# A transformer layer with Strassen products on one core: copies of stacked left rows on every second partition, and a row of attention pieces per FFN pair

## The chip, the cores and the metric

One core of a Trainium2 chip. TensorE (PE) multiplies, VectorE (DVE) and ScalarE (ACT) work elementwise, GpSimd (POOL) and SyncE (SP) mostly issue DMA transfers; ACT issues some too. The metric is the time of one launch in microseconds (us).

## The reference

`x` is [2048, 576], with D = 576, 32 heads of 18, and an FFN of F = 4608:

```python
xn = _layernorm(x, axis=-1)
return x + _A_ref(xn, A_wqkv, A_wo) + _B_ref(xn, B_w1, B_b1, B_w2, B_b2)
# _A_ref: each row s attends to rows s, s-2, ..., s-14 (W, dil = 8, 2) of its head, softmax, then @ wo
# _B_ref: relu(xn @ w1 + b1)**2 @ w2 + b2
```

Everything is float32.

## The kernel before

**Numbers.** TensorE takes the operands as pairs of a high part and a low part; each product is the sum of three (high·high, high·low, low·high). ACT makes the high part by a copy, DVE the low part by a subtraction.

**Blocks.** The 2048 rows are four blocks of 512, taken in two pairs: half `s` = 0 holds blocks 0 and 1, half `s` = 1 blocks 2 and 3. The first FFN product (and QKV) of two blocks is made by seven products in place of eight: sums and differences of weight blocks (the tiles `w1s`) times sums and differences of x (`SS`, printed as `S`, and `X`). A "pair" `p` is two of the 36 tiles of 128 FFN columns; each half has 18 pairs (`NP`), and `ffn_pair(s, p, work)` writes one of them out. `phase_a(0)` and `phase_a(1)` run the pairs of a half; within a pair stand, at fixed places, the seven products (L698, output `p`), some products with w2 of a pair before (`work`, L590), the splitting of weights into high and low (`w2s`, `w1s`), and the sums that turn seven products into four results (`r`, `h`). After `phase_a(1)`, `phase_blocks` makes the second FFN product of the odd pairs in 28 steps (L1514), and `phase_b1` the rest.

**Left rows.** 576 is four times 128 and 64 over. For pairs 0 to 2 (`PLAIN` = 3) the 64 left rows are multiplied on their own (`left`, L704, with the last slot of `w1s`). From pair 3 on, the product of the left rows is one matmul of 128 partitions more for each of the seven ("stacked"): 32 high rows and 32 low rows of x, each row twice, against the weights' high and low rows, each twice in another order, so that the 128 partitions hold the pairings of high and low. `left_x` makes x's rows and stores them in a scratch array in DRAM, `stscr[s]`, printed as `stk`: 64 rows, high and low in turn (`2 * NS * TB` from one high row to the next). `load_stack` (its transfer is L636) brings them into spare tiles: for `s` = 0 into `kv`, `xf` and `x4d`, for `s` = 1 into two buffers of `w1r`, of 4 and 3 of the seven places. Each call starts two transfers of 64 partitions: the first fills partitions 0 to 63 with the 64 rows, the second partitions 64 to 127 with the same rows. `left_w` makes the weights' rows and stores them in `lw` (L652): first 32 high rows, then 32 low rows; `load_left_weights` (L663) reads each of those 64 rows twice in succession onto 128 partitions.

**Queues.** SP issues the stack loads, the loads of `lw` and of w2 (`w2r`) and the stores; in `phase_a(1)` ACT issues the loads of `w1s` (L536, two transfers to a pair, 1024 and 768 KB), one pair ahead of use, into three buffers.

**Attention.** It has 16 items (four blocks by four groups), each a generator of 19 steps: four times a product (`pr<-q,kv`) and a reduction (`lg<-pr`), then the maximum and its subtraction (`mx`, `lg<-lg,mx`), after which the generator stops with "exp"; then the exponential on ACT (L414); the sum, reciprocal and scaling (`sm`, `lg<-lg,sm`); then four times a product (`pr<-lg,kv`) and a step of three additions (`pr<-pr` twice and `q<-pr`). Nearly all of it is on DVE. The order of every engine's instructions is the order in which the program is written, and `side(k)` puts the next k steps at the place where it is called. Three tables say how many: `PIECES[p]`, one number for each pair of `phase_a(0)`, all at the pair's start; `SPOTS[p]`, six numbers for each pair of `phase_a(1)`, one for each of its places (`spot(0)` to `spot(5)`); `LAST[k]` after step k of `phase_blocks`. In `phase_a(1)` the number is added to `owed`, and steps are run until less than half a step is owed or an "exp" is met; what an "exp" stops is owed to the next place. Places 2 and 3 of a pair lie beside its two sums `r<-p,r`, on which the next products wait.

Of the kernel before, what the change touches and what calls it, by code (L numbers as in the profile page):

```python
# [8 lines left out]
F32 = mybir.dt.float32  # L9
# [7 lines left out]
P = 128  # L17
S, D, F = 2048, 576, 4608
H, DH, W, DIL = 32, 18, 8, 2
TB = 512  # L20
# [5 lines left out]
G = 4  # L26
# [6 lines left out]
L = P // G  # L33
# [9 lines left out]
NS = 7  # L43
PLAIN = 3
ROWS = {(4 * b - 1 + k // 3, k % 3): (b, h) for b in (2, 3) for k, h in ((0, 0), (2, 2), (3, 1), (5, 2), (6, 2))}
PIECES = (0, 0, 0, 2, 3, 4, 0, 3, 2, 0, 2, 2, 1, 0, 2, 2, 4, 5)
SPOTS = ('000001',) + ('110022', '110023', '110023', '110023') * 4 + ('110021',)
QUADS = ('01111110111110', '10100010101011', '00110111111111', '10010000111111', '00000000000001', '00110010101010')
LAST = '0000000000000111001010111111'
SINGLES = '12121212121200000000'  # L50
PAIRED = tuple(range(1, 16, 2))
SINGLE = tuple(p for p in range(NP) if p not in PAIRED)
# [7 lines left out]
def block_kernel(ctx: ExitStack, tc: tile.TileContext, x, xt, wqkv, wo, w1, b1, w2, b2, w1l, w2q, w2l, out):  # L60
    nc = tc.nc
# [53 lines left out]
    stscr = [dram.tile([2 * L, NS, TB], F32, name=f"stk{s}") for s in range(2)]  # L115
    lwscr = [dram.tile([G, 2, L, NS * P], F32, name=f"lw{i}") for i in range(-(-NP // G))]
# [10 lines left out]
    def tt(out, a, b, op):  # L127
        return nc.vector.tensor_tensor(out=out, in0=a, in1=b, op=op)  # L128
# [312 lines left out]
    def side(k, exp=True):  # L441

        while k > 0:
            if current[0] is None:
                if not queue or queue[0][0] not in landed:
                    return k
                name, make = queue.pop(0)
                current[:] = [make(), None, name]
                steps_done[0] = 0
            if current[1] == "exp" and not exp:  # L450
                return k
            try:
                current[1] = next(current[0])
                steps_done[0] += 1
                k -= 1
            except StopIteration:
                current[0] = None
        return 0
# [3 lines left out]
    def some_side(t):  # L462
        owed[0] += t
        while True:
            exp = current[1] == "exp"
            cost = COST[steps_done[0]] if current[0] is not None else COST[0]
            if owed[0] < cost / 2 or side(1):
                break
            owed[0] -= cost
            if exp or current[1] == "exp":  # L470
                break
# [128 lines left out]
    def dims(t, off, *ap):  # L600
        a = t[tuple(slice(0, 1) for _ in t.shape)]
        return bass.AP(tensor=a.tensor, offset=a.offset + off, ap=[*ap])

    def high_low(v, store):
        lo, hi = v[:, :NS], v[:, NS:]
        yield
        nc.scalar.activation(hi.bitcast(F32R), lo, AF.Copy)
        yield
        tt(lo.bitcast(F32R), lo, hi, ALU.subtract)
        store(0, hi)  # L610
        store(1, lo)
        yield
# [20 lines left out]
    def load_stack(s, t, i):  # L633
        n = min(t.shape[1], NS - i)
        for h in range(2):
            nc.sync.dma_start(t[2 * h * L:2 * (h + 1) * L, :n].bitcast(F32), stscr[s][:, i:i + n])  # L636
        for k, place in STACK.items():
            if i <= place < i + n:
                ST[k] = t[:, place - i]
# [5 lines left out]
    def left_w(i):  # L645
        v = rv.pop(("w", i))
        w = lambda k: v[:, STACK[k]]
        tt(w(T3), w(B22), w(T1), ALU.subtract)
        tt(w(T1), w(T1), w(B11), ALU.subtract)
        tt(w(T2), w(B22), w(T1), ALU.subtract)  # L650
        tt(w(T4), w(B21), w(T2), ALU.subtract)
        yield from high_low(v, lambda k, part: (nc.gpsimd if i else nc.sync).dma_start(  # L652
            dims(lwscr[i], k * L * NS * P, [NS * P, L], [2 * L * NS * P, G], [1, NS * P]), part.rearrange("p s c -> p (s c)")))

    def load_left_weights(s, p):
        place = (p - PLAIN) % 2 + 1 if not s else (p - PLAIN) % 3
# [16 lines left out]
    def ffn_pair(s, p, work, first=False):  # L673
# [32 lines left out]
        def part(i):  # L706
# [15 lines left out]
            if i == 2 - p and p in (1, 2) and s:  # L722
                load_stack(1, sb.tile([P, 4, TB], F32R, name="w1r", bufs=2), 4 * p - 4)
            if i == 2 and p == PLAIN - 1 and not s:
                load_stack(0, mt.tile([P, 1, TB], F32R, name="x4d"), 6)
# [7 lines left out]
            if (p, i) == (1, 2):  # L733
                load_stack(0, sb.tile([P, 5, TB], F32R, name="kv", bufs=3), 0)
                load_stack(0, sb.tile([P, 1, TB], F32R, name="xf"), 5)
            r = p // G + 1
            if i == 1 and p % G == 1 and G * r < NP:
                load_left_w(r, sb.tile([P, 2 * NS, P], F32, name="st"))
            elif p % G == 2 and G * r < NP:
                if i == 0:  # L740
                    rv["of", r] = left_w(r)
                next(rv["of", r])
# [50 lines left out]
        def spot(i):  # L793
            if s and (not first or i == 5):
                some_side(int(SPOTS[p][i]))

        if not first and not s:
            side(PIECES[p], False)
        spot(0)
# [276 lines left out]
    def load_h(s, p):  # L1076
        t = hs[s, p] = mt.tile([P, 2, 2, TB], F32R, name="h", bufs=3)
        nc.sync.dma_start(t[:, 1].rearrange("p f t -> p (f t)").bitcast(F32), hscr[s][p])
# [6 lines left out]
    def h_lo(s, p):  # L1085
        if p < NP:
            t = hs[s, p]
            tt(t[:, 1], t[:, 1].bitcast(F32), t[:, 0].bitcast(F32), ALU.subtract)
# [415 lines left out]
    def phase_blocks():  # L1504
# [28 lines left out]
        for k in range(len(ORDER)):  # L1533
# [54 lines left out]
            if k == 25:  # L1588
                load_h(1, SINGLE[1])
                h_hi(1, SINGLE[0])  # L1590
                h_lo(1, SINGLE[0])
            side(int(LAST[k]))
        load_h(1, SINGLE[2])
# [253 lines left out]
    def q0():  # L1847
# [59 lines left out]
        for j in range(NJ):  # L1907
# [5 lines left out]
            if j in (0, 2):  # L1913
                some(parts, 2)
        of_w = left_w(0)
        hi(B11, b11)
        some(parts, 2)
# [174 lines left out]
```

## Time and profile before

| | |
|---|---|
| time before, median of 3 runs | 1099.99 us (1099.34 to 1100.98) |
| the profiled execution's own time | 1099.84 us |
| its span in the trace | 1098.1 us |
| TensorE busy | 99% of the span |
| VectorE busy | 85% |
| ScalarE busy | 52% |
| GpSimd busy | 15% |
| moved by DMA | 312.53 MB, mean 285 GB/s |

The span is from the first to the last event that the profiler saw, 1.74 us less than the execution's own time. Busy shares are averages over the whole span. The list of waits says for each engine which instructions stood still and what ended the wait; the windows give each engine's busy time, the clock granted to TensorE (PEclk, 1.00 is full speed) and the DMA rate in a stretch of the span; the timeline gives single instructions with their start, their duration and, in brackets, the idle time before them and what ended it. Consecutive instructions of one kind stand in one row (x6) with the time of all of them.

### The profile page before, as it was taken

How to read it: one execution, taken by the hardware profiler on the slowest of the kernel's cores; microseconds unless marked ns; L12 is line 12 of the kernel's file. 1: busy time of each engine (PE TensorE's matmuls, PEld its weight loads, DVE VectorE, ACT ScalarE, POOL GpSimd, SP SyncE). 2: the span in 40 equal slices, each digit the busy share in tenths (PEclk: the TensorE clock that was granted, in tenths of full speed). 3: DMA queues.
4: the chain of work that ended last, by engine and by line, in shares of the span. 5: the costliest groups of instructions: out<-in, count | busy, mean ns of one | idle time of the engine just before them, and what ended most of it. 6: DMA issues, size and time to landing. Idle time of an engine off the chain costs nothing.

```text
span 1098.1 us, 13935 instructions
## 1 busy us (share of the span) xinstructions
PE 1083.5 (99%) x4871; PEld 908.9 (83%) x4871; DVE 930.9 (85%) x1245; ACT 570.7 (52%) x800; POOL 160.0 (15%) x294
## 2 busy tenths in 40 slices
PE   9999999999999999999999998999999999999998
PEld 7998888888888888888799986888778888887887
DVE  7976899999988979999899676879688888888986
ACT  5545655666656564555344344555455555543332
POOL 5011220212130100003110301021021040000110
PEclk9999999999999999999999999999999999999999
DMA  8758997897998697876865989998988988566573
GB/s 284 256 198 304 302 403 275 320 356 285 328 342 311 222 387 238 282 247 219 304 219 164 359 299 308 383 334 333 377 291 327 361 322 313 177 206 213 203 235 100
DMA packets 106887, 312.53 MB, mean 285 GB/s; under 512 B 12865, under 2 KB 39489, under 8 KB 95169
## 3 DMA queue, kind: packets, MB, share of 16 engines
q1 hardware_dynamic: 70048, 198.75, 51.5%
q0 software_dynamic: 15584, 71.96, 18.0%
q10 hardware_dynamic: 21184, 40.94, 11.1%
q8 instruction: 38, 0.62, 0.2%
q14 instruction: 33, 0.26, 0.1%
HBM read 216.62 MB, written 94.98 MB: 284 GB/s over the span
## 4 chain that ended last, share of the span: by engine, by line
PE 90%; DVE 5%; DMA 3%; issue 1%; ACT 1%; POOL 0%; ACTq 0%; DVEq 0%; POOLq 0%
PE p L590 35%; PE p L698 34%; PE p L1187 9%; PE p L1514 6%; PE p L1843 2%; DMA w1s<-w 2%; PE p L1191 2%; DVE pr L128 1%; PE p L1898 1%; PE p L704 1%; DMA w2r<-in_wo 1%; DVE h L128 1%; PE p L1753 1%; DVE w2s L128 0%; DVE r L128 0%
## 5 line engine op out<-in xcount | busy, mean ns | idle before, releaser
L590 PE MATMUL p<-h,w2s 128*128 128x512 f32 x1618 | 389.6, 390 | 0.0
L590 PEld LDWEIGHTS p<-h,w2s 128*128 128x128 f32 x1618 | 303.7, 188 | 64.3 <-ACT h L749 0.5
L698 PE MATMUL p<-X,w1s 128*128 128x512 f32 x864 | 219.6, 390 | 1.5 <-DVE r L128 1.5
L698 PEld LDWEIGHTS p<-X,w1s 128*128 128x128 f32 x864 | 162.2, 188 | 35.8 <-DVE r L128 1.9
L698 PE MATMUL p<-S,w1s 128*128 128x512 f32 x648 | 167.2, 394 | 0.5 <-ACT p L786 0.5
L698 PEld LDWEIGHTS p<-S,w1s 128*128 128x128 f32 x648 | 121.1, 189 | 29.3 <-ACT r L806 2.9
L562 ACT ACTIVATE w2s<-w2r 128x640 fp32r<-128x640 f32 x132 | 96.7, 734 | 87.2 <-PE p L590 54.1
L434 POOL DMA_DIRECT2D o<-q x128 | 69.4, 620 | 466.3 <-DVE q L128 465.8
L128 DVE TENSOR_TENSOR w2s<-w2r,w2s 128x576 fp32r<-128x576 f32 (+1 forms) x133 | 99.8, 751 | 18.0 <-ACT w2s L562 17.8
L745 ACT ACTIVATE r<-r,b1t 128x512 f32<-128x512 f32 x72 | 52.1, 724 | 116.1 <-DVE r L128 114.1
L128 DVE TENSOR_TENSOR h<-h 128x1024 fp32r<-128x1024 f32 (+1 forms) x74 | 72.5, 989 | 21.3 <-ACT h L762 13.7
L128 DVE TENSOR_TENSOR pr<-lg,kv 128x1152 f32<-128x1152 f32 x64 | 86.7, 1355 | 1.3
L128 DVE TENSOR_TENSOR pr<-q,kv 128x1152 f32<-128x1152 f32 x64 | 86.7, 1355 | 1.1
L405 DVE TENSOR_REDUCE lg<-pr 128x64 f32<-128x1152 f32 x64 | 86.4, 1350 | 1.0
L128 DVE TENSOR_TENSOR r<-p,r 128x512 f32<-128x512 f32 (+2 forms) x81 | 55.0, 681 | 36.2 <-ACT r L831 18.2
L128 DVE TENSOR_TENSOR pr<-pr 128x576 f32<-128x576 f32 (+1 forms) x128 | 77.5, 605 | 3.1
L753 ACT ACTIVATE r<-r 128x1024 f32<-128x1024 f32 x56 | 59.2, 1057 | 0.9
L806 ACT ACTIVATE r<-p 128x512 f32<-128x512 f32 x36 | 21.5, 598 | 57.2 <-PE p L698 57.1
L128 DVE TENSOR_TENSOR w1s<-w1r,w1s 128x1024 fp32r<-128x1024 f32 (+2 forms) x42 | 46.2, 1102 | 5.6 <-ACT w1s L523 5.0
L831 ACT ACTIVATE r<-p 128x512 f32<-128x512 f32 x36 | 21.5, 599 | 54.1 <-PE p L698 54.1
L745 ACT ACTIVATE r<-p,b1t 128x512 f32<-128x512 f32 x72 | 48.2, 671 | 0.0
L128 DVE TENSOR_TENSOR h<-r,h 128x1024 fp32r<-128x1024 f32 (+2 forms) x35 | 39.9, 1146 | 7.6 <-ACT r L753 6.0
(263 smaller groups left out, 1488.2 us busy)
## 6 DMA issues: line engine op xcount, KB each, us to landing
kv<-kvq POOLq DMA_DIRECT2D x32, 1296.0 KB, 9.6
w2r<-in_w SPq DMA_DIRECT2D x112, 320.0 KB, 4.1
w<-w1s SPq DMA_DIRECT2D x21, 1024.0 KB, 7.1
w1s<-w ACTq DMA_DIRECT2D x19, 1024.0 KB, 8.0
h<-r SPq DMA_DIRECT2D x28, 512.0 KB, 6.5
h<-h SPq DMA_DIRECT2D x28, 512.0 KB, 4.0
w<-w1s SPq DMA_DIRECT2D x15, 768.0 KB, 9.4
w1s<-w ACTq DMA_DIRECT2D x15, 768.0 KB, 7.7
```

Of the source, the lines that this page charges most:

```text
L128: return nc.vector.tensor_tensor(out=out, in0=a, in1=b, op=op)
L405: nc.vector.tensor_reduce(out=lg[:, j * HG:(j + 1) * HG].rearrange("p a w -> p w a"), in_=pr.rearrange("p w (a d) -> p w a d", d=DH), axis ...
L434: nc.gpsimd.dma_start(rows[:, i], q[i * L:(i + 1) * L, :, a:z])
L562: nc.scalar.activation(w2s[stream[i]][:, :DE], raw2[i], AF.Copy)
L590: nc.tensor.matmul(yp[b][c], v, a, start=c not in yb[b], stop=c in last and c not in [o[0] for o in ops[i + 1:]], skip_group_check=True)
L698: nc.tensor.matmul(to, l, r, start=start and i == 0, stop=i == len(mm) - 1, skip_group_check=True)
L745: nc.scalar.activation(to, a, AF.Relu, bias=b1t[:, f:f + 1])
L753: nc.scalar.activation(r, r, AF.Square)
L1187: nc.tensor.matmul(to, l[:, js], r, start=start and n == 0, stop=n == len(mm) - 1, skip_group_check=True)
L1191: nc.tensor.matmul(to, v[:, js], ws[LEFT, f][:, n], start=False, stop=n == 1, skip_group_check=True)
L1514: nc.tensor.matmul(p, l, r, start=id(p) not in begun, stop=stop, skip_group_check=True)
L1843: nc.tensor.matmul(p[:, :QW], l, r, start=k == 0, stop=k == len(mm) - 1)
```

## The change

The transfers of `load_stack` are put together in another way. The first now takes the 32 high rows and writes each of them to two neighbouring places of every second partition (0, 2, 4, ...), the second the 32 low rows to partitions 1, 3, 5, ... A transfer still covers 64 partitions with the same bytes, but its partitions now span all 128. The weights' rows are stored high and low in turn, so that the same rows meet in the matmul; the loads of `lw` are as before. The products are the same, in another order of the 128 rows.

Besides, three tables of attention's steps change: pair 14 of `phase_a(0)` gets one step more, `SPOTS` has a row of its own for each pair in place of four rows repeated, and step 22 of `phase_blocks` gets none.

```diff
-PIECES = (0, 0, 0, 2, 3, 4, 0, 3, 2, 0, 2, 2, 1, 0, 2, 2, 4, 5)
-SPOTS = ('000001',) + ('110022', '110023', '110023', '110023') * 4 + ('110021',)
+PIECES = (0, 0, 0, 2, 3, 4, 0, 3, 2, 0, 2, 2, 1, 0, 3, 2, 4, 5)
+SPOTS = ('000002', '110022', '110023', '010023', '110023', '110022', '110023', '100024', '010024', '120022', '110023', '110023', '110023', '110022', '110023', '110023', '110123', '010021')
...
-LAST = '0000000000000111001010111111'
+LAST = '0000000000000111001010011111'
...
     def load_stack(s, t, i):
         n = min(t.shape[1], NS - i)
         for h in range(2):
-            nc.sync.dma_start(t[2 * h * L:2 * (h + 1) * L, :n].bitcast(F32), stscr[s][:, i:i + n])
+            nc.sync.dma_start(t[h::2, :n].rearrange("p s c -> p (s c)").bitcast(F32),
+                              dims(stscr[s], h * NS * TB + i * TB, [2 * NS * TB, L], [0, 2], [1, n * TB]))
...
         yield from high_low(v, lambda k, part: (nc.gpsimd if i else nc.sync).dma_start(
-            dims(lwscr[i], k * L * NS * P, [NS * P, L], [2 * L * NS * P, G], [1, NS * P]), part.rearrange("p s c -> p (s c)")))
+            dims(lwscr[i], k * NS * P, [2 * NS * P, L], [2 * L * NS * P, G], [1, NS * P]), part.rearrange("p s c -> p (s c)")))
```

How the instructions stand on SP's queue around the second half's stack (`stk_151` is its scratch array), before:

```order
L551 DMA w2r<-in_w 128x640
L636 DMA w1r<-stk_151 64x2048 x2
L663 DMA st<-lw_152 128x1x896
L636 DMA w1r<-stk_151 64x1536 x2
L766 DMA op_157<-h 128x2048
```

and of the change:

```order
L551 DMA w2r<-in_w 128x640
L636 DMA w1r<-stk_151 64x1x2048 x2
L664 DMA st<-lw_152 128x1x896
L636 DMA w1r<-stk_151 64x1x1536 x2
L767 DMA op_157<-h 128x2048
```

Nothing moves: the four transfers keep their places and sizes, and only the partitions they write and the rows they read differ.

On VectorE, from the last part of pair 9 of `phase_a(1)` into pair 10 (`r_6718` and `r_6717` are pair 9's two sums, as `r_6720` and `r_6719` are in the change; `h<-h x2` finishes pair 9 in the course of pair 10), before:

```order
L128 TENSOR_TENSOR w2s<-w2r,w2s 128x576
L128 TENSOR_TENSOR r_6718<-p_6659,r_6698 128x512
L411 TENSOR_REDUCE mx<-lg 128x32
L128 TENSOR_TENSOR lg<-lg,mx 128x256
L128 TENSOR_TENSOR r_6717<-p_6659,r_6698 128x512
L128 TENSOR_TENSOR h<-h 128x512 x2
L416 TENSOR_REDUCE sm<-lg 128x32
L417 RECIPROCAL sm<-sm 128x32
L128 TENSOR_TENSOR lg<-lg,sm 128x256
L128 TENSOR_TENSOR pr<-lg,kv 128x1152
L128 TENSOR_TENSOR pr<-pr 128x576
L128 TENSOR_TENSOR pr<-pr 128x288
```

and of the change:

```order
L411 TENSOR_REDUCE mx<-lg 128x32
L128 TENSOR_TENSOR lg<-lg,mx 128x256
L128 TENSOR_TENSOR w2s<-w2r,w2s 128x576
L128 TENSOR_TENSOR r_6720<-p_6659,r_6698 128x512
L128 TENSOR_TENSOR r_6719<-p_6659,r_6698 128x512
L416 TENSOR_REDUCE sm<-lg 128x32
L417 RECIPROCAL sm<-sm 128x32
L128 TENSOR_TENSOR lg<-lg,sm 128x256
L128 TENSOR_TENSOR pr<-lg,kv 128x1152
L128 TENSOR_TENSOR pr<-pr 128x576
L128 TENSOR_TENSOR pr<-pr 128x288
L128 TENSOR_TENSOR q<-pr 128x144
```

The maximum with its subtraction has moved ahead of the first sum of pair 9, and the sum, reciprocal and scaling with the first product and additions have moved from behind the first `h<-h x2` of pair 10 to ahead of it.

On VectorE in `phase_blocks`, around its steps 21 to 23 (`X_7720`, and `X_7722` in the change, is one sum of outputs; the `w1s<-w1s` is the low part of an operand that a later step takes), before:

```order
L128 TENSOR_TENSOR X_7720<-X_7720 128x1024
L128 TENSOR_TENSOR h<-h 128x1024
L128 TENSOR_TENSOR w1r<-X_7720,w1r 128x1024
L128 TENSOR_TENSOR w2s<-w2r,w2s 128x576
L128 TENSOR_TENSOR pr<-pr 128x576
L128 TENSOR_TENSOR pr<-pr 128x288
L128 TENSOR_TENSOR q<-pr 128x144
L128 TENSOR_TENSOR w1s<-w1s 128x1024
```

and of the change:

```order
L128 TENSOR_TENSOR X_7722<-X_7722 128x1024
L128 TENSOR_TENSOR h<-h 128x1024
L128 TENSOR_TENSOR w1r<-X_7722,w1r 128x1024
L128 TENSOR_TENSOR w2s<-w2r,w2s 128x576
L128 TENSOR_TENSOR w1s<-w1s 128x1024
```

The step of three additions no longer stands ahead of the low part; the place of step 20 holds additions where it held a product of attention.

## The prediction

> **What bounds the kernel now.** I read the shares first, then the list of what TensorE waits for, then the windows around its longest waits, then the timeline inside them.
>
> ```profile
> PE 1083.5 (99%) x4871; PEld 908.9 (83%) x4871; DVE 930.9 (85%) x1245; ACT 570.7 (52%) x800; POOL 160.0 (15%) x294
> ```
> ```profile
> PE p L704 <- DMA w1s<-w: 4.0, 1, 4.0
> ...
> PE p L698 <- DVE r L128: 1.5, 1, 1.5
> PE p L1514 <- DVE w1s L128: 0.7, 1, 0.7
> PE p L698 <- ACT p L786: 0.5, 1, 0.5
> ```
>
> TensorE is busy all but 1% of the span, and the change takes no matmul away. So it can only win where TensorE stands still or runs at a lower clock. Four waits (total us, times, longest us) lie where the change acts: one on a DMA, 4.0 us, and three on DVE or ACT, 2.7 us together. Those at the start, between the halves and at the end lie elsewhere, and I leave them as they are.
>
> The long wait is in the third pair of the second half (pair 2), which is the last one before the stacked rows are used:
>
> ```profile
> 664.16 1.52 PE L698 MATMUL p<-S,w1s 128*128 128x512 f32 x6
> 669.71 0.72 PE L704 MATMUL p<-x,w1s 128*128 128x512 f32 x2 [4.03 <-DMA w1s<-w]
> ```
> ```profile
> 655.71 0.33 ACTq L536 DMA_DIRECT2D w1s<-w  x1
> ```
> ```profile
> w1r<-stk SPq DMA_DIRECT2D x2, 512.0 KB, 14.8
> ```
> ```profile
> 130.00:136.00 6.00, 6.00 (x28) 4.95 (x28) 5.80 (x11) 4.53 (x7) 0.00 (x0) 1.00 0.97 215
> 140.00:147.00 7.00, 7.00 (x32) 5.80 (x31) 6.72 (x12) 4.43 (x6) 0.55 (x1) 1.00 1.02 421
> 543.00:546.00 3.00, 3.00 (x17) 2.88 (x16) 2.96 (x6) 1.35 (x2) 0.00 (x0) 1.00 0.88 330
> 658.00:665.00 7.00, 7.00 (x32) 5.80 (x32) 4.49 (x7) 4.53 (x6) 0.00 (x0) 1.00 1.05 221
> 665.00:670.00 5.00, 0.97 (x5) 0.51 (x4) 4.93 (x8) 0.60 (x1) 0.00 (x0) 1.00 1.00 308
> 670.00:674.00 4.00, 4.00 (x12) 3.10 (x12) 0.02 (x1) 0.00 (x0) 0.00 (x0) 0.57 1.04 259
> ```
>
> The weights that L704 needs are issued at 655.71 and land as the wait ends, at 669.7. In between stand the stack loads (`w1r<-stk`, 14.8 us each to landing). The last three columns of a window are the granted clock, the DMA share and GB/s. While stack loads are in flight (658 to 665, and 130 to 136 in the first half) the engines are as busy as ever, 1.05 and 0.97, but move only 221 and 215 GB/s; from 140 to 147, with other loads, a share of 1.02 moves 421. **A stack load onto 64 neighbouring partitions runs at half the rate.** After the wait TensorE's clock is 0.57 for 4 us, a loss of 4 × 0.43 = 1.72. So the place costs 4.03 + 1.72 = 5.75 us.
>
> [...]
>
> ```profile
> 542.57 1.44 PE L1187 MATMUL p<-r,X 128*128 128x432 f32 x6 [2.04 <-DVE h L1063]
> ```
>
> **The stack's copies.** Number of transfers, bytes and queue places stay. What can change is the rate, and what each row reads: every DRAM row is still read twice, now in succession, as the loads of `lw` do already:
>
> ```profile
> mb<-lw SPq DMA_DIRECT2D x13, 448.0 KB, 5.6
> ```
>
> 448 KB land in 5.6 us there, so reading twice is not slow in itself. From 658 to 669.7 the queues moved 221 × 7 + 308 × 4.7 = 2995 KB. At 421 GB/s these take 7.1 us, and the weights land at 665.1. TensorE is ready for them at 664.16 + 1.52 = 665.68. The wait goes, with 0.6 us in hand, and the clock loss with it: **−5.75**. The break-even rate is 2995 / 7.68 = 390 GB/s. The loads queued behind it come some 4.6 us sooner, and TensorE 5.75 sooner, so the next one loses about 1 us of its lead. The two ends of this term: nothing at 221 GB/s, 5.75 at 390 or above. I take the upper one, nearest to the row of 421.
>
> [...] The slow windows agree with the half rate; no row here has a strided transfer.
>
> The weights' rows leave in the same stores with another step in DRAM, off TensorE's path, and the matmuls are the same: 0.
>
> **Pairs 9 to 11.** A step of attention is a product (1.36), a reduction, or three additions (1.25 + 0.31 = 1.56).
>
> ```profile
> 785.35 1.42 DVE L128 TENSOR_TENSOR h<-h 128x512 f32<-128x512 f32 x2 [4.80 <-ACT h L762]
> 787.97 1.36 DVE L128 TENSOR_TENSOR pr<-lg,kv 128x1152 f32<-128x1152 f32 x1
> 789.36 1.25 DVE L128 TENSOR_TENSOR pr<-pr 128x576 f32<-128x576 f32 x2
> 790.64 0.31 DVE L128 TENSOR_TENSOR q<-pr 128x144 f32<-128x144 f32 x1
> 790.87 1.28 DVE L128 TENSOR_TENSOR h<-h 128x512 f32<-128x512 f32 x2
> 793.34 0.75 DVE L128 TENSOR_TENSOR w2s<-w2r,w2s 128x576 fp32r<-128x576 f32 x1
> 794.01 0.68 DVE L128 TENSOR_TENSOR r<-p,r 128x512 f32<-128x512 f32 x1
> ```
> ```profile
> 791.53 1.75 PE L590 MATMUL p<-h,w2s 128*128 128x512 f32 x7
> 794.75 1.66 PE L698 MATMUL p<-X,w1s 128*128 128x512 f32 x6 [1.47 <-DVE r L128]
> 802.37 1.65 PE L698 MATMUL p<-S,w1s 128*128 128x512 f32 x6 [0.53 <-ACT p L786]
> ```
>
> DVE stood idle for 4.80 us, then had softmax's scaling, two products and additions between its `h` and the sum `r` that TensorE waits for. Of the change, scaling, product and additions stand ahead of 785.35, where that idle time takes them. What is left: 1.42 + 1.36 + 1.28 + 1.56 + 0.75 + 0.68 = 7.05, done at 792.4; TensorE comes at 791.53 + 1.75 = 793.28. So the 1.47 goes, and the 0.53 of pair 11, which descends from it; the first six matmuls after each wait took 1.66 and 1.65 for 1.52, another 0.27: **−2.27**.
>
> What moves ahead is met in pair 9:
>
> ```profile
> 766.15 0.69 DVE L128 TENSOR_TENSOR r<-p,r 128x512 f32<-128x512 f32 x1
> 770.80 1.22 DVE L128 TENSOR_TENSOR h<-r,h 128x1024 fp32r<-128x1024 f32 x1
> 777.23 0.42 DVE L128 TENSOR_TENSOR lg<-lg,mx 128x256 f32<-128x256 f32 x1
> 778.07 1.52 PE L698 MATMUL p<-X,w1s 128*128 128x512 f32 x6
> ```
> ```profile
> L405 DVE TENSOR_REDUCE lg<-pr 128x64 f32<-128x1152 f32 x64 | 86.4, 1350 | 1.0
> ```
>
> From 766.84 DVE has three products and three reductions (8.13), the `h` (1.22), maximum and subtraction (0.84), the low part (0.75) and the sum (0.69): 11.63 without the gaps, so 778.47. TensorE comes at 778.07: a new wait of **+0.4**. Between nothing (ACT or the gaps give it back) and 0.84 (all of the moved step), I take the sum.
>
> **The other places.** In `phase_blocks`:
>
> ```profile
> 1003.85 1.22 DVE L128 TENSOR_TENSOR w1s<-w1s 128x1024 fp32r<-128x1024 f32 x1
> 1005.13 1.42 PE L1514 MATMUL p<-w1s,w1r 128*128 128x512 f32 x5 [0.66 <-DVE w1s L128]
> ```
>
> The additions (1.56) leave from ahead of the low part, so its wait goes, −0.66; at step 20 the additions stand for a product, 0.2 more, which I count in full: **−0.46**. In pair 16 of the second half a product (1.36) comes ahead of the second sum:
>
> ```profile
> 883.78 0.69 DVE L128 TENSOR_TENSOR r<-p,r 128x512 f32<-128x512 f32 x1
> 888.02 0.58 ACT L786 ACTIVATE p<-p 128x512 f32<-128x512 f32 x1
> 889.93 1.52 PE L698 MATMUL p<-S,w1s 128*128 128x512 f32 x6
> ```
>
> ACT's chain behind that sum then ends its copy `p<-p` at 888.60 + 1.36 = 889.96, just as TensorE comes for it: **+0.1**, between 0 and 1.4. Pair 14 of the first half gets the maximum and subtraction (0.84) one pair sooner, and the following pairs have it less; DVE's spare 15% hides it, 0, at most 0.84. The remaining moves of a step by one place even out within a pair, 0, each bounded by its 1.36 either way.
>
> **Sum:** −5.75 − 2.27 − 0.46 + 0.4 + 0.1 = −7.98. From the profiled execution's 1099.84 this is **1091.8**; the median of the runs, 1099.99, is 0.15 above that execution, which I neglect.
>
> **Rivals.**
>
> *The rate rises by a part only.* Sixteen engines share 64 rows, four each. If an engine takes four rows in succession, they now lie on eight neighbouring partitions, and engines that work in step could still meet on the same part of the memory. At 300 GB/s the weights land at 658 + 10.0 = 668.0: a wait of 2.3 without clock loss, so 1091.8 + 2.3 = **1094.1**; at 270 it is 3.4 and the clock is at stake, 1095.2 to 1096.9. For it: the limit lies in something that several partitions share, as the full engine share at half rate shows, and the stride only spreads rows over it. Against it: the spread is even over a whole transfer.
>
> *The change doesn't do what it says.* If DRAM reads of the scratch rows set the 221, or the engines stay in step, the term is 0, and what is left is the tables': −2.23, **1097.6**. For it: both slow windows read the same kind of scratch. Against it: `mb<-lw` reads such rows at no such cost.
>
> *A new wait on DVE takes the rest.* The rows of `SPOTS` were set for a program with the old wait in pair 2; that wait gave DVE and the loads some 6 us of lead. Without it a sum or a load a few pairs later may be late by 2 to 4: about **1095**. For it: DVE is 85% busy, and pair 9 already comes out late by 0.4. Against it: from pair 3 on, 4.80 us of idle time in pair 10 absorb a shift.
>
> *Slower.* If strided rows halve the rate once more, the 1547 KB of 658 to 665 take 14 us in place of 7: the weights land 7 us later, the clock loss stays, 1099.84 + 7 − 2.23 = **1104.6**. It decides from a loss of 4.4 us on, that is under 1547 / 11.4 = 136 GB/s. For it: two neighbouring copies of one row now read DRAM in short succession. Against it: `mb<-lw`, and the row size on either side is unchanged.
>
> **How the numbers follow.** Full rate 0.52, part of it 0.20, no gain in rate 0.17, new wait 0.06, slower 0.05. Forecast 1091.8. The full-rate case alone reaches from 1090.0 (the +0.5 of pairs 9 and 16 and the 0.2 of step 20 do not come, and the loads behind give 1 us) to 1093. With the part rate and the new wait the range is **1090.0 to 1097.2**; outside lie most of the third case and the last. About 0.2%, 2.2 us, is what a measurement can tell from no change. The first, second and fourth cases lie under 1097.8; 1097.6 sits at the border, and half of its 0.17 counts as faster. Faster 0.86, same 0.09, slower 0.05.
>
> **What would show it.** Right: the wait at L704 under 0.5 us, no clock below 1.00 in the 4 us behind it, the stretch after the stack loads' issue at 400 GB/s or more, and `w1r<-stk` landing in under 11 us; no wait of pair 10 on `r`; the `w1s` wait of `phase_blocks` gone; a new wait of about 0.4 in pair 9. Wrong: 215 to 221 GB/s again while only stack loads are in flight, a wait of 4 us on `w1s<-w`, or a new wait of over 1 us on `r` or `p` in the second half.

## The result, and the profile after

The changed kernel takes 1089.88 us (median of 4 runs, 1088.06 to 1090.64) where the kernel before took 1099.95 (4 runs, 1099.34 to 1100.98): a ratio of 0.9905, with a 95% interval of 0.9888 to 0.9922. The forecast was 1091.8 with a range of 1090.0 to 1097.2. The direction was right and the gain, 10.1 us where 8.0 were forecast, was underestimated, so that the time lies 0.1 us below the range. The profiled execution of after is the fastest of the four, 1088.06 us with a span of 1086.3.

The shares of the page, and the list of what TensorE waits for:

```profile
PE 1080.5 (99%) x4871; PEld 908.2 (84%) x4871; DVE 932.3 (86%) x1245; ACT 571.2 (53%) x800; POOL 160.3 (15%) x294
```
```profile
PE p L1671 <- DVE lg L1664: 2.1, 1, 2.1
```

Of TensorE's waits in before one is left, that at the start. (Line numbers behind `load_stack` are one higher in the changed kernel, so L704 is L705.) Pair 2 of the second half in the timeline, TensorE, then the queues of ACT and SP:

```profile
661.89 1.52 PE L699 MATMUL p<-S,w1s 128*128 128x512 f32 x6
663.25 0.61 PE L705 MATMUL p<-x,w1s 128*128 128x512 f32 x2
```
```profile
651.44 0.60 ACT L832 ACTIVATE r<-p 128x512 f32<-128x512 f32 x1 [2.12 <-PE p L699]
651.44 0.33 ACTq L536 DMA_DIRECT2D w1s<-w  x1
```
```profile
651.46 3.53 SPq L636 DMA_DIRECT2D w1r<-stk  x2
```

The two matmuls of L705 come without a wait. The list of DMA issues (us to landing last) and the windows (granted clock, DMA share, GB/s last) show the rate:

```profile
w1r<-stk SPq DMA_DIRECT2D x2, 512.0 KB, 9.9
```
```profile
655.00:658.00 3.00, 3.00 (x15) 2.49 (x14) 2.23 (x4) 1.54 (x3) 0.00 (x0) 1.00 0.99 415
658.00:661.00 3.00, 3.00 (x15) 2.46 (x15) 1.91 (x3) 2.40 (x4) 0.00 (x0) 1.00 1.02 421
661.00:665.00 4.00, 4.00 (x19) 3.34 (x18) 3.21 (x6) 1.88 (x3) 0.00 (x0) 1.00 1.03 419
665.00:670.00 5.00, 5.00 (x23) 4.14 (x23) 4.90 (x9) 1.90 (x3) 0.00 (x0) 1.00 1.00 419
```

Where 221 GB/s moved before, 415 to 421 move now; the clock stays at 1.00. Pair 10 (the sum `r` and the matmuls behind it), pair 9, pair 16 (with ACT's copy between the two) and `phase_blocks`, each DVE first, then TensorE:

```profile
783.44 0.68 DVE L128 TENSOR_TENSOR r<-p,r 128x512 f32<-128x512 f32 x1
785.23 1.52 PE L699 MATMUL p<-X,w1s 128*128 128x512 f32 x6
```
```profile
769.28 0.68 DVE L128 TENSOR_TENSOR r<-p,r 128x512 f32<-128x512 f32 x1
770.02 1.66 PE L699 MATMUL p<-X,w1s 128*128 128x512 f32 x6
```
```profile
874.64 0.68 DVE L128 TENSOR_TENSOR r<-p,r 128x512 f32<-128x512 f32 x1
878.88 0.58 ACT L787 ACTIVATE p<-p 128x512 f32<-128x512 f32 x1
879.51 1.65 PE L699 MATMUL p<-S,w1s 128*128 128x512 f32 x6
```
```profile
991.79 1.22 DVE L128 TENSOR_TENSOR w1s<-w1s 128x1024 fp32r<-128x1024 f32 x1
993.52 1.52 PE L1515 MATMUL p<-w1s,w1r 128*128 128x512 f32 x6
```

In pair 10 the sum ends 1.1 us before TensorE asks for it. In pair 9 the sum, and in pair 16 ACT's copy behind the sum, ends just late enough (0.06 and 0.05 us before TensorE starts) to slow the six matmuls behind it (1.66 and 1.65 in place of 1.52), a loss of 0.1 to 0.3, too short to be listed as a wait.

TensorE runs the same 4871 matmuls in the same order in both kernels. So the start of each matmul in one trace can be subtracted from that of the same matmul in the other; the steps of that difference say where the time went:

| place | forecast, us | trace before to trace after, us |
|---|---|---|
| between the halves (L1187) | none | -2.3 |
| second half, pair 2 | -5.75 | -5.9 |
| pair 9 | +0.4 | +0.3 |
| pairs 10 and 11 | -2.27 | -2.5 |
| pair 16 | +0.1 | +0.1 |
| `phase_blocks` | -0.46 | -1.0 |
| all else | 0 | -0.5 |
| sum | -7.98 | -11.8 |

The largest departure from the forecast, 2.3 us, stands where the change does nothing.

### The profile page after: what moved, and what is told of

It reads as the page before. It is cut to its first block, busy times and chain, and to the rows that moved or that the text cites. A ratio compares the mean times of both kernels' runs of the same rounds, so it can differ in the third digit from the quotient of the medians.

```text
span 1086.3 us, 13933 instructions
## 1 busy us (share of the span) xinstructions
PE 1080.5 (99%) x4871; PEld 908.2 (84%) x4871; DVE 932.3 (86%) x1245; ACT 571.2 (53%) x800; POOL 160.3 (15%) x294
## 4 chain that ended last, share of the span: by engine, by line
PE 97%; DVE 2%; DMA 0%; issue 0%; ACT 0%; POOL 0%; POOLq 0%
PE p L590 38%; PE p L699 35%; PE p L1188 9%; PE p L1515 8%; PE p L1844 2%; PE p L1192 2%; PE p L1899 1%; PE p L705 1%; PE p L1754 1%; DVE lg L405 0%; DVE pr L128 0%; DMA kv<-in_x 0%; DVE st L155 0%; DVE r L128 0%; PE p L1716 0%; PE p L1653 0%
```

## The experiments

The first four kernels, on one chip, ask which part of the change brings what, and whether the wait between the halves belongs to it. The kernel before took 1099.64 us beside them (median of 22).

**The stack alone.** The `load_stack` and `left_w` of the change, with the tables of before:

```diff
-            nc.sync.dma_start(t[2 * h * L:2 * (h + 1) * L, :n].bitcast(F32), stscr[s][:, i:i + n])
+            nc.sync.dma_start(t[h::2, :n].rearrange("p s c -> p (s c)").bitcast(F32),
+                              dims(stscr[s], h * NS * TB + i * TB, [2 * NS * TB, L], [0, 2], [1, n * TB]))
```

> The kernel before with the new stack transfers and weight rows alone, the three tables as before. Theory A (the rate of the stack loads made the wait of pair 2): 5 to 6.5 us faster than before, about 1094.2; the wait of L704 on w1s gone, no clock below 1.00 behind it, over 400 GB/s behind the issue of the stack loads; the waits of pairs 10 and 11 (1.5 and 0.5) and of phase_blocks (0.7) still there. Theory B (the tables issue pair 2's weights sooner, and that removed the wait): less than 3 us faster, a wait of over 2 us left on w1s.

Measured: 1092.73 us (1092.21 to 1093.66), ratio 0.9939 [0.9925, 0.9952], 6.9 us less, a little more than theory A's 5 to 6.5. What TensorE waits for:

```profile
PE p L699 <- DVE r L128: 1.5, 1, 1.5
PE p L699 <- ACT p L787: 1.2, 2, 0.7
PE p L1515 <- DVE w1s L128: 0.7, 1, 0.7
PE p L1188 <- DVE h L1064: 0.6, 1, 0.6
```

The wait on `w1s<-w` is gone and the other three stay, as theory A said. One of the two waits on ACT's `p`, 0.7 us, stands at the start of pair 15, behind the second sum of pair 14; the first trace of before doesn't have it.

**The tables alone.** `PIECES`, `SPOTS` and `LAST` of the change, with the stack transfers of before.

> The kernel before with the three new tables alone, the stack transfers as before. Theory A: 2.2 to 3.5 us faster, about 1097; the waits of pairs 10, 11 and phase_blocks gone, the wait of L704 on w1s still 3.5 us or more with the clock below 0.7 behind it, stack windows at 215 to 225 GB/s. Theory B: 6 us or more faster, with the wait of L704 under 1 us although the stack loads are as slow as before.

Measured: 1095.02 us (1092.55 to 1099.67, 11 runs), ratio 0.9964 [0.9949, 0.9978]: 4.6 us less, more than theory A allowed and less than theory B asked. The profiled execution was the fastest one:

```profile
PE p L698 <- ACT r L806: 1.5, 1, 1.5
PE p L698 <- DMA mb<-lw: 1.4, 1, 1.4
PE p L1514 <- DVE h L128: 0.4, 1, 0.4
```
```profile
658.00:661.00 3.00, 3.00 (x15) 2.49 (x14) 1.78 (x3) 2.21 (x4) 0.00 (x0) 1.00 1.06 244
661.00:665.00 4.00, 4.00 (x19) 3.30 (x19) 3.15 (x6) 1.94 (x3) 0.00 (x0) 1.00 1.01 256
```

The stack loads are nearly as slow as before, and yet L704 doesn't wait, as theory B had it. New waits of 1.4 and 1.5 us stand in pair 4, the first of them on the left rows of the weights. The reason is in the queues. In the first trace of before ACT's queue stands until the first load of pair 2's `w1s` has landed, and issues the second one only then (from the chain that ended last):

```profile
647.81 7.82 DMA w1s<-w
...
655.71 13.96 DMA w1s<-w
```

That is 2.0 us after ACT's copy at the end of pair 1 begins (653.71), and 3.3 us behind the first stack transfer (652.37). In the kernels with the tables the second load is issued with the copy, as the rows of after above show, while the first is still in flight. There it is SP's queue that stands for that landing, ahead of the second stack transfer (in after):

```profile
SPq L636 <- DMA w1s<-w: 2.3, 1, 2.3
```

**Before and after again**, unchanged, for second traces.

> The kernel before, unchanged, for a second trace. Theory A (the wait of L1187 between the halves, 2.04 us in the first trace of before and absent in that of after, comes and goes from execution to execution): this or the next kernel's trace shows it otherwise than the first trace of the same kernel did. Theory B (the change removes it): 1.8 to 2.2 us here again. Time 1099 to 1101 by both.

> The changed kernel, for a second trace and more times. Theory A: 1089 to 1091; the trace has a wait of 0 to 2.2 us at L1188 on the sums of h between the halves, and executions with and without it make the spread of 2.6 us of the times so far. Theory B: no such wait here either, and the spread has another cause.

Measured: 1098.89 us for before (10 runs, 1098.35 to 1102.29), 1089.53 for after (6 runs, 1088.53 to 1093.64; ratio 0.9906 [0.9892, 0.9921]). The second trace of before, then of after:

```profile
PE p L704 <- DMA w1s<-w: 3.7, 1, 3.7
...
PE p L1187 <- DVE h L1063: 1.8, 1, 1.8
PE p L698 <- DVE r L128: 1.5, 1, 1.5
PE p L698 <- ACT p L786: 0.9, 2, 0.5
PE p L1514 <- DVE w1s L128: 0.7, 1, 0.7
```
```profile
PE p L1188 <- DVE h L1064: 2.1, 1, 2.1
...
PE p L1515 <- DVE h L128: 0.8, 1, 0.8
```

The changed kernel has the wait between the halves here, and hadn't in its first trace. Over the twelve traces of this case it lies between 0 and 2.1 us, in kernels with the new parts and without them. It goes with the moment at which a load of `wo` lands: at 537.5 us in the first trace of after, without a wait, and at 540.7 in the second, with 2.1. So 2.3 of the 11.8 us (the wait and the slower matmuls around it) are chance, and so is part of the spread of the times. That leaves 9.5 us in the first two traces for the change. The second trace of after also has a wait of 0.8 us on `h` at the head of `phase_blocks`, behind a load (`h<-op`), and the place costs 1.0 us. Such a wait, of 0.4 to 0.8 us, is listed in three of the nine traces of kernels with pair 0's new number and in none of the three others; whether the tables cause it isn't shown.

**What sets the stack's rate.** The change alters two things in a transfer: the partitions that it writes and the order in which it reads. Two kernels separate them. In both, rows of x meet other rows of the weights than they should, so the left rows' products are others; the transfers' sizes and places are those of the change. The first writes neighbouring partitions:

```diff
-            nc.sync.dma_start(t[h::2, :n].rearrange("p s c -> p (s c)").bitcast(F32),
+            nc.sync.dma_start(t[2 * h * L:2 * (h + 1) * L, :n].rearrange("p s c -> p (s c)").bitcast(F32),
                               dims(stscr[s], h * NS * TB + i * TB, [2 * NS * TB, L], [0, 2], [1, n * TB]))
```

> The changed kernel, but each stack transfer fills 64 neighbouring partitions (0 to 63 with the high rows, 64 to 127 with the low ones), still reading each row twice in succession; the rows meet other rows of the weights, so the left rows' products are others. Theory P (the partitions written set the rate): the stack windows at 215 to 260 GB/s, the 512 KB transfers 11 us or more to landing, waits behind pair 3 as with the tables alone, about 1095. Theory R (the order of reading sets it): 400 GB/s or more, about 1089.5.

The second writes every second partition and reads as before:

```diff
-            nc.sync.dma_start(t[h::2, :n].rearrange("p s c -> p (s c)").bitcast(F32),
-                              dims(stscr[s], h * NS * TB + i * TB, [2 * NS * TB, L], [0, 2], [1, n * TB]))
+            nc.sync.dma_start(t[h::2, :n].bitcast(F32), stscr[s][:, i:i + n])
```

> The changed kernel, but both stack transfers read the 64 rows in the order before (high and low in turn, all of them in each transfer) and write them to every second partition; again other pairings, other products of the left rows. Theory P: 400 GB/s or more behind the issue, landing of the 512 KB in 9 to 11 us, 1089 to 1090.5. Theory R: 215 to 260 GB/s and about 1095.

Measured: neighbouring partitions 1095.13 us (1093.05 to 1096.08), every second partition 1090.05 (1088.53 to 1091.74). The stack's issue and a window of each, neighbouring first:

```profile
w1r<-stk SPq DMA_DIRECT2D x2, 512.0 KB, 11.4
```
```profile
661.00:665.00 4.00, 4.00 (x20) 3.30 (x19) 2.44 (x4) 2.69 (x4) 0.00 (x0) 1.00 1.00 233
```
```profile
w1r<-stk SPq DMA_DIRECT2D x2, 512.0 KB, 9.0
```
```profile
661.00:665.00 4.00, 4.00 (x19) 3.34 (x18) 2.06 (x3) 2.50 (x4) 0.00 (x0) 1.00 1.01 409
```

233 GB/s against 409, at a full share of the engines in both: the partitions written set the rate, and the order of reading makes no difference of note (409 read once, 419 read twice in succession, in the same window of after). With it the rival that the rate comes from reading the scratch rows falls.

**What the tables do in pair 2.** One number of the kernel before is changed:

```diff
-SPOTS = ('000001',) + ('110022', '110023', '110023', '110023') * 4 + ('110021',)
+SPOTS = ('000002',) + ('110022', '110023', '110023', '110023') * 4 + ('110021',)
```

> The kernel before with one number changed: pair 0 of SPOTS gives 2 steps at its last place in place of 1, so all of attention in the second half runs a step earlier. Theory Q (that step, a product of 1.36 us ahead of the low part of w2s, holds back SP's w2 load and so the stack loads behind it by about 1 us; the first w1s load of pair 2 then lands before them and the second is issued 2 us sooner): the w1s load directly behind ACT's copy at the end of pair 1, the wait of L704 under 0.5 us at the old rate of the stack loads, but new waits of 1 to 4 us in pairs 3 to 5, where the weights' left rows come late; 2 to 5 us faster than before. Rival S (other rows of the tables did it): the wait of L704 3.5 us or more as before, within 1.5 us of before.

> The tables alone once more, for a second trace, since the first one was of the fastest of eleven executions (1092.6, median 1095.0). Theory Q: L704 waits under 1 us again, and 3 us or more are lost in pairs 3 to 5 behind slow stack loads. If the first trace was an exception, L704 waits 2 us or more.

Measured beside 1099.69 for before (median of 24): 1098.11 us for the one number (12 runs, 1096.72 to 1105.1), ratio 0.9991 [0.9976, 1.0006], so no difference that can be told; 1095.23 for the tables again (8 runs, 1093.99 to 1100.4), ratio 0.9970 [0.9953, 0.9986]. The queue of ACT and the waits for the one number:

```profile
652.84 0.60 ACT L831 ACTIVATE r<-p 128x512 f32<-128x512 f32 x1 [2.12 <-PE p L698]
652.85 0.33 ACTq L536 DMA_DIRECT2D w1s<-w  x1
```
```profile
PE p L698 <- DMA mb<-lw: 4.9, 1, 4.9
...
PE p L698 <- DMA w1s<-w: 1.9, 2, 1.2
PE p L698 <- ACT p L786: 1.5, 1, 1.5
```

and the waits of the tables again:

```profile
PE p L698 <- DMA mb<-lw: 2.4, 1, 2.4
...
PE p L698 <- DMA w1s<-w: 0.7, 1, 0.7
```

Theory Q was right that the single number does it and about what follows, and wrong about the gain and about a part of the cause. With one product of attention (1.36 us) more ahead of DVE's low parts at the end of pair 0, SP's next w2 load waits longer for its buffer, and the stack loads stand behind it. Against TensorE's own progress they are issued 1.4 us later in after than in before, and the second `w1s` load 2.0 us sooner. But the first `w1s` load doesn't have to land ahead of them for that: in after it lands at 654.4, and the stack loads start at 651.46. What changes is which transfer waits for that landing. In all three traces with the old number the second `w1s` load is issued within 0.1 us behind it, in all nine with the new number the second stack transfer is. The packed traces have the semaphore: the one that the first `w1s` load raises (109) is raised next by the second `w1s` load in before, and by the second stack transfer in after. How one step more leads to another order of semaphores, no run here shows.

So L704 doesn't wait although the loads are slow. But the slow loads now delay the weights' left rows (`mb<-lw`): TensorE waits for them 4.9 us in pair 4 with the one number, 1.4 and 2.4 in the two traces of the tables, and with the other losses right behind, the place costs 7.2, 3.5 and 4.3 us. The wait of 4 us hadn't gone; it had moved. Rival S, under which L704 would still wait 3.5 us, falls.

**Two halves of the tables, on top of the stack.** First the stack's change with that one number (the other rows, `PIECES` and `LAST` as before):

> The new stack transfers and, of the tables, one number alone (pair 0 gives 2 steps at its last place). Theory U (a step more by pair 0 is what takes the scaling ahead of the sums in pairs 9 and 10, and the other rows only guard pair 14 and phase_blocks): the waits of pairs 10 and 11 gone as in the changed kernel, no wait on the weights' left rows, a wait of 0.4 to 0.7 in phase_blocks and 1 to 1.6 on ACT's p in pair 14; 1091 to 1092.5. Rival V (the other rows carry the gain): pairs 10 and 11 wait 2 us or more, 1092.5 or above. If the rows changed nothing but the first: 1089.5.

then the changed kernel with the old `LAST`:

> The changed kernel with the old LAST (step 22 of phase_blocks runs a step of attention again, which is then one of those the end would have run). Theory: a wait of 0.4 to 0.7 on the low part w1s at L1515 comes back, with slower first matmuls behind it, and phase_blocks takes 0.6 to 1.0 us longer: 1090.2 to 1090.8. Rival (the step does not matter there once the pairs before run earlier): 1089.3 to 1089.9, no wait over 0.3.

Measured beside a median of 1100.47 for before: 1093.71 us (1092.9 to 1094.28), ratio 0.9942 [0.9930, 0.9955], and 1090.37 us (1089.86 to 1091.18), ratio 0.9911 [0.9896, 0.9926]. The waits of the first, then of the second:

```profile
PE p L699 <- ACT p L787: 2.1, 2, 1.5
...
PE p L1515 <- DVE w1s L128: 0.4, 1, 0.4
PE p L699 <- DVE r L128: 0.3, 1, 0.3
```
```profile
PE p L1515 <- DVE w1s L128: 0.4, 1, 0.4
PE p L1515 <- DVE h L128: 0.4, 1, 0.4
```

With the one number the 1.5 us of pairs 10 and 11 are gone and there is no wait on `mb<-lw`, but 1.5 us at the start of pair 15 and 0.3 and 0.5 in pairs 4 and 5 take their place. The time is no better than with the stack alone (0.9939). So theory U holds for pairs 10 and 11, but the time is above its 1092.5, since pairs 4 and 5 weren't in it. Rival V has the time right and the waits of pairs 10 and 11 wrong: running a step earlier everywhere moves the bad spots, and only the other rows remove the new ones. The old `LAST` brings back the wait of `phase_blocks` on `w1s`. From the first trace of after to this one, `phase_blocks` takes about 1.0 us more from step 22 on (0.7 at the waiting product, 0.3 some sixteen matmuls later). The wait on `h` isn't the old `LAST`'s: the second trace of after has it too. The times can't tell the difference: the ratios are 0.9911 and 0.9906, with intervals of some 1.6 us each way, and the runs of before beside them differ by 0.8.

## Why the prediction was off

**The stack's copies: right in the mechanism.** Forecast -5.75; from the first trace of before to the first of after -5.9, to that of the stack alone -5.6, and from the second trace of before to the stack alone -6.3 (there the clock was 0.85 from 665 to 670 and 0.50 from 670 to 674, against 1.00 and 0.57 in the first trace). The rate went from 221 to 420 GB/s, the wait and the loss of clock went. Measured by itself the part is worth 6.9 us (5.3 to 8.2 by the interval). The forecast's 0.6 us in hand weren't there: with the stack alone the weights are issued at 654.57 and take 9.7 us to land, just as TensorE comes for them at 664.29. In the changed kernel they land at 659.4, 3.9 us ahead of L705, since they are issued sooner as well. So each part alone takes this wait away, the stack's with nothing in hand. The half rate belongs to the neighbouring partitions, as the forecast had it, and not to the reading of the scratch rows. From 661 to 665 us 233 GB/s moved onto neighbouring partitions and 419 onto every second one where each row is read twice in succession, 409 onto every second one where the rows are read as before. No row of the prediction has a load of 64 partitions that lie apart; that such a load would move the 421 of other loads, the upper end of the term, was an estimate of mine, and 409 to 421 is what the runs showed for it.

**Pairs 9 to 11 and 16: right.** -2.5 for -2.27 in pairs 10 and 11, +0.3 for +0.4 in pair 9, +0.1 for +0.1 in pair 16.

**The step that failed is the sum of the tables, -2.23, and with it the floor of 1090.0.** On top of the stack the tables brought 3.2 us by medians (1092.73 to 1089.53), 1.0 more. Two terms were too small. In `phase_blocks` I counted -0.66 for the wait and 0.2 in full against it, -0.46 together. The 0.2 never came, and the matmuls behind the wait run at their usual pace too: both pairs of traces of before and after say -1.0 there. And the "remaining moves of a step", set at 0, hold a wait at the start of pair 15 on ACT's `p`. The second trace of before has 0.4 us there, that of the stack alone 0.7; none of the traces with all of the new tables has it. The first trace of before didn't show it, and I took one execution's list of waits for the kernel's. The forecast had no term either for the wait on `h` at the head of `phase_blocks`, which in the second trace of after takes the 1.0 us back; so how the 1.0 us by medians divides stays open.

The other half of the miss of 2.1 us stands, by medians, at the stack: 6.9 against 5.75. That lies within its interval, and the traces have 5.6 to 6.3; so it can't be called a mis-sized term.

**The floor was also too close by its own logic.** It let the new costs vanish and gave the loads 1 us. It had no room for a wait that comes and goes, such as the one at L1187 (0 to 2.1 us), which I had set aside as lying elsewhere. Part of why the stack alone is worth 6.9 by medians and 5.6 to 6.3 in the traces stays open: that wait was smaller in its trace (0.6) than in both of before (2.0 and 1.8), and nothing ties it to the stack.

**What the forecast missed without harm.** It said that the transfers' places in the queues stay, which is true of the order and not of the time. Pair 0's extra step alone removes the wait at L704, by changing which load waits for which landing. Had the rate not risen, L704 would still have run without a wait, and the forecast would have been right about that pair for the wrong reason. The tables alone gain 4.6 us by medians, the stack 6.9, both 10.1: the parts together are 1.4 us above the whole. That fits, within intervals of some 1.5 us each way: both remove pair 2's 5.9 us, and with the tables alone the slow loads take about 3.5 of it back in pair 4 (trace of the tables alone against that of after), which leaves an overlap of 2.4.

**The rivals.** The part rate and "the change doesn't do what it says" fall with 420 GB/s; a new wait of 2 to 4 us a few pairs later didn't come; nor did the slower rate.

## What to carry to other kernels

Loads onto 64 neighbouring partitions ran at 215 to 256 GB/s here with all engines busy, and the same bytes on every second partition at 409 to 421; where rows must be copied twice onto 128 partitions, as here, interleave the copies. A wait that an issue's moment decides can be moved away by a single step on another engine (4.0 us at L704), and may turn up at the next thing behind the slow load (4.9 us in pair 4): look for it there before counting it as gained, and look at what the queue itself waited for before it issued the load. And one trace's list of waits is a sample: a second trace of the same kernel tells which of them to build a floor on.

## What was not expected of the hardware

In the second trace of after TensorE's clock fell behind a wait of 2.1 us (the row of TensorE and two windows, granted clock third from the end):

```profile
543.19 2.43 PE L1188 MATMUL p<-r,X 128*128 128x432 f32 x6 [2.14 <-DVE h L1064]
```
```profile
541.00:544.00 3.00, 0.86 (x4) 0.75 (x4) 2.37 (x4) 0.99 (x2) 0.00 (x0) 0.89 0.48 164
544.00:547.00 3.00, 3.00 (x10) 2.79 (x9) 2.93 (x6) 1.34 (x2) 0.00 (x0) 0.54 0.93 363
```

The six matmuls took 2.43 us where 1.44 were needed behind the wait of 2.04 in the first trace of before, at a clock of 1.00. So a wait of about 2 us cost its own length in one execution (2.04 us) and some 1.4 us more in another (2.14 us, then 3 us at 0.54). The wait of 2.3 us that the rival of the part rate counts without a loss of clock was an estimate, between a wait of 2.04 at 1.00 and one of 4.03 followed by 0.57, and no run shows it; the waits on either side of it are these 2.14 us, and 2.44 in pair 4 of the second trace of the tables, behind which six matmuls took 2.35 us in place of 1.52.
